# Where the expert sums, dots and weight loads stand around a phase change, in a fused attention and product-key expert kernel

## The chip, the cores and the metric

The kernel runs on one core of a Trainium2 chip. The metric is the device time of one execution in microseconds. The core has a matrix engine (PE, whose weight loads are shown as PEld), a vector engine (DVE), an activation engine (ACT), GpSimd (POOL, which issues the indirect gathers here) and SyncE (SP, which issues nearly all other transfers). Each engine takes its instructions in the order in which they were recorded, and waits on semaphores for the others.

## The reference

Two branches read the same layer-normed tokens, and their outputs are added to the input: attention with 32 query heads of width 16 on one shared key and value head, and a product-key expert layer. There are 2048 tokens of width 512.

```python
def _A_ref(x, wq, wk, wv, wo):
    q = (x @ wq).reshape(B, S, 32, 16).transpose(0, 2, 1, 3)
    k = x @ wk
    v = x @ wv
    p = softmax(einsum("bhqd,bkd->bhqk", q, k) * 16 ** -0.5)
    return einsum("bhqk,bkd->bhqd", p, v) -> (B, S, 512) @ wo

def _B_ref(x, w_q, k1, k2, u, v):
    q = einsum("nd,dhc->nhc", xf, w_q)          # 32 heads, 2 x 128 wide
    s1, s2 = q[..., :128] @ k1.T, q[..., 128:] @ k2.T   # 64 scores each
    i1, i2 = top 2 of s1, top 2 of s2           # 4 candidate pairs
    top_s, top_e = best 2 of the 4 sums         # expert i1 * 64 + i2 of 4096
    g = softmax(top_s)
    act = gelu(einsum("nd,nhkd->nhk", xf, u[top_e]))
    return einsum("nhk,nhk,nhkd->nd", g, act, v[top_e])

xn = layernorm(x)
return x + _A_ref(xn, ...) + _B_ref(xn, ...)
```

So each token meets 64 experts (32 heads, 2 each). An expert needs a row of u for a dot with the token, a gelu, and a row of v for a weighted sum.

## The kernel before

**Tokens.** The 2048 tokens stand in four groups of 512 (phases 0 to 3), each of four tiles of 128. The 32 expert heads are taken in eight chunks of four.

**Attention** is the backbone. 256 double steps, counted by `d`, each do for one unit (a block of 512 queries and four heads) two key tiles: four score tiles (`scores`, L326, and the exp on ACT, L329) and two `pv` products (L340). Into each double step the kernel puts two kinds of other work, by `att_steps(d, mid, fill)`.

**The search** is the filler on PE (`fill`). `score_thread` is a generator that walks the list `SEQ` of (phase, chunk): all chunks of phase 0, two chunks of phase 1, all of phase 2, the other six of phase 1, all of phase 3. `item` scores one token tile against one chunk: twelve matmuls into a PSUM tile `psc` (L531), then on DVE eight MAX8 (L544) and eight index finds (L546), which free that tile. `psc`, `pw`, `pwt`, `pact`, `pout`, `pwo`, `pg` and `ptd` share three PSUM buffers. Each `yield` gives a cost in planned microseconds, and `run_scores` takes steps until the plan (`aim`, growing evenly over the double steps) is met.

**Chunk weights.** In phase 0, beside the search of chunk n, `wp_make` builds the weights of chunk n + 1: per head a raw tile `wqt` is loaded by SP (`wp_load`), multiplied by the keys (`pw`, L486), copied by ACT, and transposed by PE (`pwt`, L493); ACT makes the high part (L495), DVE the low part `wk` (L496), which also frees the transpose's PSUM tile. The weights are stored to DRAM (`dw`) and read back in later phases (`wp_read`). Where the phase changes, the four tiles `xt` of transposed tokens are reloaded by SP during the last token tile of the old phase (`load_phase2_xt`).

**Slots (phases 0 and 1).** For these tokens the experts' rows are gathered: 512 slots, each a POOL gather `g` of 128 rows of u and v together (L970), a dot on DVE with the tokens (`dots`, L982) and a weighted sum on DVE into the token's accumulator `xa` (`adds`, L1017). For each four slots there is a chain of three small operations on DVE (`gq`, `gy`, `ga`; the list `CHAIN`), a tanh on ACT (`gth`, L998) and a weight on DVE (`w`, L1005). Twelve buffers hold gathers (`NGB`), two of them lent at times to the output weights (`lent`). A sum frees its gather buffer, and the next gather may start.

**Dense groups (phases 2 and 3).** For these tokens all 4096 experts are multiplied on PE, in 32 blocks (`dense`). The gates of the found experts are spread from one-hot products: `batch` makes `da` tiles of indices and gates (the gates come last, after an exp on ACT: `den`, L635, to `da`, L643, put into the list `BEHIND`), PE transposes them (`ptd`, L752), DVE makes one-hots (L777 to L780) and PE multiplies these (`pg`, L809). Then each block has `pact` (L727), an activation, and `pout` (L855). `dense_on` tells the stage: 4 at the last token tiles of the search ahead of a dense group, 2 for the one-hots, 3 and 1 for the blocks.

**The order by hand.** The loop over d sets how many dots are recorded in this double step: `pos` grows by a rate that depends on the stage, and `todo` is what is due, as far as gathers were issued. `mid`, recorded between the attention products of the double step, has in this order: the tanhs that are ready, the ACT lists, the dots (with one weight ahead of the last dot), and then `go`: the sums, the rest of `BEHIND` (`rest`) and `CHAIN` in turn, and up to four gathers. `fill` follows: the search's steps of that double step. While `dense_on` is 2, `go` is recorded after the filler instead (`POST_FILL`), with the chain at once. `quiet` counts double steps in which no sum is recorded; before, only the end of the one-hots set it.

Of the kernel before, what the change touches and what calls it, by code (L numbers as in the profile page):

```python
# [11 lines left out]
F32 = mybir.dt.float32  # L12
# [11 lines left out]
P = 128  # L24
# [31 lines left out]
def tile_kernel(ctx, tc, x, wq, wkv, wo, wqT, kT, uv, ub, vb, out):  # L56
# [408 lines left out]
    def wp_load(c, h):  # L465
        if late[0] is None or (c == 1 and h < 2):
            w = gtile(F32, (P, 2, D), "wqt") if c == 0 and h > 1 else big.tile([P, 2, D], F32, name="wqt", tag="wqt", bufs=2)
        else:
            w = late[0].tile([P, 2, D], F32, name="wqt", tag="gy", bufs=3)
        nc.sync.dma_start(w, wqT[4 * c + h].rearrange("(s p) d -> p s d", p=P))  # L470
        WC["raw", c, h] = w

# [3 lines left out]
    def wp_make(c):  # L476

        wt = [big.tile([P, 2, 512], F32, name="wt", tag="da", bufs=2) for _ in range(2)]
        for h in range(4):
            for n in range(4 * c + h + 1, min(4 * c + h + 3, 4 * NC) if late[0] else 4):  # L480
                if ("raw", n // 4, n % 4) not in WC:
                    wp_load(n // 4, n % 4)
            w = WC.pop(("raw", c, h))
            p = xtile("pw")
            for s in range(2):
                nc.tensor.matmul(p[s * E:(s + 1) * E, :], kTs[:, s, :], w[:, s, :], start=True, stop=True)  # L486
            nc.scalar.copy(wt[h // 2][:, h % 2, :], p)
            yield 0.9
        WC[c] = []
        for k in range(KC):  # L490
            p = xtile("pwt")
            for h in range(4):
                nc.tensor.transpose(p[:, h * P:(h + 1) * P], wt[h // 2][:, h % 2, k * P:(k + 1) * P], ident)  # L493
            wk = wk_tile()
            nc.scalar.copy(wk[:, 0, :], p)  # L495
            nc.vector.tensor_tensor(out=wk[:, 1, :], in0=p, in1=wk[:, 0, :], op=OP.subtract)  # L496
            WC[c].append(wk)
            store(lambda k=k, wk=wk: nc.sync.dma_start(d_w[c][:, k], raw(wk[:])))
            yield 0.45
# [12 lines left out]
    def item(n_, ti, make=()):  # L512
        ph, c = SEQ[n_]
        nph, nc_ = SEQ[n_ + 1] if n_ + 1 < len(SEQ) else (None, None)
        t = TPH * ph + ti
        g, j = divmod(t, GT)
        b, jb = divmod(ti, BT)
        if jb == 0:
            m8 = small.tile([P, BT, 8, 8], F32, name="m8", bufs=1)
            i8 = small.tile([P, BT, 8, 8], U32, name="i8", bufs=1)  # L520
            M8[ph, c, b], I8[ph, c, b] = m8, i8
        m8, i8 = M8[ph, c, b], I8[ph, c, b]
        p = xtile("psc")

        last = ti == TPH - 1
        more = nc_ is not None and not (ph >= NSP and c == NC - 1)
        read = more and n_ + 1 >= NC
        n = 0
        for k in range(KC):
            for a, bb in TERMS:  # L530
                nc.tensor.matmul(p, XT[g][k][:, a, j * P:(j + 1) * P], WC[n_][k][:, bb, :],  # L531
                                 start=n == 0, stop=n == 11)
                n += 1
            if read and ti == 0 and k < 2:
                wp_read(n_ + 1, range(2 * k, 2 * k + 2))
            if last and more and nph != ph:
                load_phase2_xt(nph, k)
            if k < KC - 1:
                yield 3 * UNIT
            if k == 1:  # L540

                yield from islice(make, 1)
        for s in range(8):
            nc.vector.max(m8[:, jb, s, :], p[:, s * E:(s + 1) * E])  # L544
        for s in range(8):
            nc.vector.max_index(i8[:, jb, s, :], m8[:, jb, s, :], p[:, s * E:(s + 1) * E])  # L546
        if jb == BT - 1:
            batch(ph, c, b)
        yield 3 * UNIT
# [100 lines left out]
    def dense(DG, after):  # L650
# [211 lines left out]
        for b in range(NB):  # L862
            wd = []
            if b > 1:
                if b not in halved:

                    yield None
                if b not in halved:
                    flush()
                p = xtile("pact")  # L870
                for k in activations(b, splits[b][0], p):
                    if k == 0:
                        store(lambda b=b: fetch_gates(b + 1))
                        if b % 2 == 0 and b > 2:
                            later_split(b + 2)
                        if b == 2:

                            store(load_totals)
                    if k == KC - 1 and b == NB - 1 and after is not None:
                        wp_read(after, range(2))  # L880
                    if b == NB - 1 and after is not None:
                        load_phase2_xt(SEQ[after][0], k)
                    if k < KC - 1:
                        yield 3 * UNIT

                if b not in fetched:
                    if b > 3 and formed[0] < b - 2:
                        flush()
                    run(STORES)
                    assert b in fetched  # L890
            vs = splits.pop(b)[1]
            gy = gates[b]
            if b > 2:
                gates.pop(b - 1)
            g, y = (gy[:, 0, :], gy[:, 1, :]) if b > 1 else (gy[:, b, :], hh[:, b, :])

            def gated(g=g, p=None):
                stt(g, g, 1.0 / GS, p, op0=OP.mult, op1=OP.mult)

            def whole(y=y, g=g):  # L900
                stt(y, y, 1.0, g, op0=OP.add, op1=OP.mult)

            def scaled(y=y, g=g):
                multiplied[0] += 1
                stt(g, g, 1.0 / GS, y, op0=OP.mult, op1=OP.mult)

            def high(y=y if b > 1 else g, wd=wd):
                wd.append(late[0].tile([P, 2, 512], F32R, name="wd", tag="wd", bufs=4))
                nc.scalar.copy(wd[0][:, 0, :], y)
                behind(lambda: low(y, wd[0]))  # L910

            def low(y, wd):
                nc.vector.tensor_tensor(out=wd[:, 1, :], in0=y, in1=wd[:, 0, :], op=OP.subtract)  # L913
                formed[0] += 1

            if b > 1:
                nc.scalar.activation(y, p, AF.Square, scale=C_CUB ** 0.5)
                stt(y, y, C_IN, p, op0=OP.add, op1=OP.mult)
                LAST.append(lambda y=y: nc.scalar.activation(y, y, AF.Tanh))
                if b == 3:  # L920

                    behind(lambda gated=gated, g=g, p=p: gated(g, p))
                else:
                    gated(g, p)
                behind(whole)
                LATER_ACT.append(high)
            else:
                LATER.append(lambda scaled=scaled, high=high: (behind(scaled), on_act(high)))
            held.append((wd, vs))
            if b > 1:  # L930
                yield 3 * UNIT
            if b == 3:
                later_split(4)
            if b == 4:
                dense_on[0] = 1
            for _ in range(b - 1 if b in (2, 3) else 0):
                if out_ready():
                    block_out()
                    yield 3.6
            if b % 2:  # L940
                if b > 1:
                    later_split(b + 2)
                if ready:
                    for _ in range(2):
                        if formed[0] < used[0] + 2:
                            yield None
                    yield from sums()
                ready, held = held, []
# [140 lines left out]
    def score_thread():  # L1089
        for n, (ph, c) in enumerate(SEQ):  # L1090
# [7 lines left out]
            for ti in range(TPH):  # L1098
                if dn and ti == 1:
                    yield next(dn)  # L1100
                if dn and ti == 2:
                    dense_on[0] = 4
                yield from item(n, ti, make)
                yield from islice(make, 1)
# [31 lines left out]
    def att_steps(d, mid, fill):  # L1136
# [41 lines left out]
        if i == STEPS + 2:  # L1178
            last_out_a(3)
            last_out_b()  # L1180
        if i >= 124 and i % 128 == 124 or i == STEPS - 30:
            lent[0] = 2
        if 128 <= i < STEPS and i % 128 == (26 if i // 128 == 2 else 10) or i == STEPS - 10:
            load_wo()
# [57 lines left out]
    with tc.manual_schedule(engines={E_.PE, E_.Activation, E_.DVE, E_.Pool, E_.SP}):  # L1242
# [3 lines left out]
        for d in range(half + 24):  # L1246
# [4 lines left out]
            if dense_on[0] == 1:  # L1251
                pos += 2.6 if d < half * 3 // 4 else max(0.0, NSL - pos) / max(half - 3 - d, 1)
            else:
                pos += (2.1 if len(IDX) < NC * TPH else 2.3 if 0 <= d - since < 12 else 1.75, 0, 1.4, 1.5, 0.5)[dense_on[0]]

            todo = max(min(int(pos + 0.001), g_next[0]) - d_next[0], 0)

            def mid():
# [23 lines left out]
                if quiet[0] > 0:  # L1282
                    quiet[0] -= 1
                    sums = 0
                if dense_on[0] == 2:
                    run(CHAIN)

                def go():
# [14 lines left out]
                        if OUTS:  # L1303
                            experts_out(OUTS.pop(0))

                if dense_on[0] == 2:
                    POST_FILL.append(go)
                else:
                    go()
# [56 lines left out]
```

## Time and profile before

| | |
|---|---|
| median of 3 runs | 1934.66 us (1933.02, 1934.66, 1942.46) |
| profiled execution | 1943.82 us, span 1942.1 us |
| mean granted TensorE clock | 0.978 |
| PE busy | 1870.5 us, 96% |
| DVE busy | 1675.0 us, 86% |
| ACT busy | 1294.5 us, 67% |
| POOL busy | 562.6 us, 29% |
| transfers | 491.11 MB, mean 253 GB/s |

Times in the rows are microseconds from the start of the span. A row of a table of stretches gives for one stretch its length, the busy time of PE, PEld, DVE, ACT and POOL with the number of their instructions, the clock granted to PE (1.00 is full speed), the busy share of the transfer engines and their rate. A row of waits names who waited, for whom, the total, the number and the longest. A row of the instructions in order of time gives start, length, engine, line, operation, tiles and count, and in brackets the idle time before it and who ended it. A group's row gives busy time and mean ns, and then the idle time before.

The double steps begin at about 139 us. Chunk weights are made until about 377, the phases change near 377, 424, 1097 and 1250 us, the search of phase 2 ends and its dense group begins near 610, and the dense group of phase 3 begins near 1437.

### The profile page before, as it was taken

What the parts mean: (1) busy time and instruction counts of PE and PEld (TensorE: products, weight loads), DVE (VectorE), ACT (ScalarE), POOL (GpSimd) and SP (SyncE); (2) the same over time, 40 slices, a digit from 0 to 9 for tenths busy, and PEclk for the clock granted to TensorE, in tenths of its full rate; (3) what the DMA queues carried; (4) which work ended last, traced back from release to release, by engine and by line L of the source; (5) the groups of instructions that cost most, each with busy time, mean ns of one, the idle gap of its engine ahead of it and who ended that gap; (6) DMA issues with size and microseconds to landing.
All of it is one profiled execution on the core that took longest, in us unless ns stands there. A gap on an engine that the chain in (4) does not pass through costs nothing.

```text
span 1942.1 us, 34774 instructions
## 1 busy us (share of the span) xinstructions
PE 1870.5 (96%) x10990; PEld 994.7 (51%) x10990; DVE 1675.0 (86%) x6717; ACT 1294.5 (67%) x1803; POOL 562.6 (29%) x536
## 2 busy tenths in 40 slices
PE   6879999999999999999999999999999999999998
PEld 4634444555554544555555554555555445555553
DVE  6627788989999986899999897999999779999994
ACT  3236666655556887778778555655578877788873
POOL 1202223222221222344344423222212124344430
PEclk9979999999999889999999999999999899999999
DMA  7857879787773667798899988777746778989882
GB/s 272 316 178 257 276 269 305 278 299 239 235 254 106 197 223 244 247 287 286 276 281 299 375 284 262 256 236 260 235 126 223 240 227 279 286 265 297 279 276 84
DMA packets 234393, 491.11 MB, mean 253 GB/s; under 512 B 93396, under 2 KB 93396, under 8 KB 234204
## 3 DMA queue, kind: packets, MB, share of 16 engines
q0 software_dynamic: 73728, 268.47, 41.8%
q1 hardware_dynamic: 159240, 219.56, 34.9%
q8 instruction: 88, 1.44, 0.3%
q10 hardware_dynamic: 1236, 0.82, 0.1%
q14 instruction: 101, 0.83, 0.1%
HBM read 427.41 MB, written 56.07 MB: 249 GB/s over the span
## 4 chain that ended last, share of the span: by engine, by line
PE 70%; DVE 17%; ACT 2%; DMA 2%; issue 1%; SPq 0%; another core or an unknown queue 0%; ACTq 0%; DVEq 0%
PE pv L340 20%; PE sc L326 14%; PE psc L531 10%; PE pact L727 9%; PE pout L855 9%; DVE i L546 5%; PE pg L809 3%; DVE m L544 3%; DVE xa L1017 3%; PE pwo L433 2%; DVE g L982 2%; ACT pt L329 2%; PE pw L486 1%; DMA wqt<-in_wqT_dram 1%; DMA wk<-dw 1%
## 5 line engine op out<-in xcount | busy, mean ns | idle before, releaser
L329 ACT ACTIVATE pt<-sc 128x1024 f32<-128x1024 f32 x1024 | 993.5, 1026 | 461.2 <-PE sc L326 413.4
L970 POOL DMA_INDIRECT g<-in_uv_dram,idx x512 | 554.7, 1083 | 1325.5 <-DVE xa L1017 670.7
L340 PE MATMUL pv<-pt,vaug 128*32 128x512 f32 x4096 | 513.1, 619 | 0.0
L531 PE MATMUL psc<-wk,xt 128*128 128x512 f32 x1536 | 390.7, 402 | 9.5 <-DVE wk L496 2.9
L326 PE MATMUL sc<-qa,kaug 64*128 64x512 f32 x2048 | 386.7, 453 | 9.6 <-ACT pt L329 8.8
L1017 DVE SCALAR_TENSOR_TENSOR xa<-g,w,xa 128x512 f32<-128x512 f32 x512 | 372.5, 746 | 0.1
L982 DVE CUSTOM_DVE_ANT_0 g<-g,xa 128x512 f32<-128x512 f32 x512 | 335.5, 682 | 6.6 <-DMA g<-in_uv_dram,idx 6.6
L531 PEld LDWEIGHTS psc<-wk,xt 128*128 128x128 f32 x1536 | 278.2, 188 | 114.5 <-issue 38.0
L326 PEld LDWEIGHTS sc<-qa,kaug 64*128 64x128 f32 x2048 | 157.0, 186 | 331.5 <-ACT pt L329 205.7
L340 PEld LDWEIGHTS pv<-pt,vaug 128*32 128x32 f32 x4096 | 109.3, 111 | 256.4 <-issue 254.8
L546 DVE FIND_INDEX8 i<-m,psc 128x8 uint32<-128x64 f32 x1024 | 206.6, 222 | 0.0
L727 PE MATMUL pact<-xt,wk 128*128 128x512 f32 x768 | 197.6, 402 | 1.5 <-DVE i L546 1.1
L855 PE MATMUL pout<-wk,wd 128*128 128x512 f32 x768 | 194.9, 402 | 0.2 <-DVE wd L913 0.2
L544 DVE MAX8 m<-psc 128x8 f32<-128x64 f32 x1024 | 146.3, 215 | 27.6 <-PE psc L531 26.1
L727 PEld LDWEIGHTS pact<-xt,wk 128*128 128x128 f32 x768 | 140.0, 189 | 51.1 <-issue 17.9
L855 PEld LDWEIGHTS pout<-wk,wd 128*128 128x128 f32 x768 | 140.8, 188 | 47.4 <-DVE act L982 4.7
L692 DVE TENSOR_TENSOR wk<-rw,wk 128x512 fp32r<-128x512 f32 x128 | 85.0, 684 | 8.0 <-ACT wk L691 8.0
L858 DVE TENSOR_TENSOR da<-da,pout 128x512 f32<-128x512 f32 x128 | 82.9, 681 | 10.1 <-PE pout L855 9.4
L777 DVE TENSOR_TENSOR oh<-oh 128x2048 f16<-128x2048 f16 x64 | 78.0, 1219 | 2.2 <-PE pg L809 2.2
L809 PEld LDWEIGHTS <-oh 128*128 128x128 f16 x1024 | 68.4, 163 | 13.1 <-issue 4.6
L809 PE MATMUL pg<-oh 128*128 128x32 f16 x1024 | 73.6, 247 | 0.4 <-DVE oh L780 0.4
L691 ACT CAST wk<-rw 128x512 fp32r<-128x512 f32 x128 | 74.0, 631 | 0.0
(156 smaller groups left out, 1286.6 us busy)
## 6 DMA issues: line engine op xcount, KB each, us to landing
wk<-dw SPq DMA_DIRECT2D x96, 512.0 KB
wqt<-in_wqT_dram SPq DMA_DIRECT2D x32, 512.0 KB
dw<-wk SPq DMA_DIRECT2D x32, 512.0 KB
rw<-in_ub_dram SPq DMA_DIRECT2D x64, 256.0 KB
rw<-in_vb_dram SPq DMA_DIRECT2D x64, 256.0 KB
gy<-dg SPq DMA_DIRECT2D x64, 256.0 KB
qa<-dqh SPq DMA_DIRECT2D x128, 64.0 KB
g<-in_uv_dram,idx POOLq DMA_INDIRECT x512
```

Source lines behind the costliest of these rows:

```text
L326: nc.tensor.matmul(p[:, b, :], kaug[o:o + 64, kc * P:(kc + 1) * P], QA[u][o:o + 64, i, :], start=True, stop=True)
L329: nc.scalar.activation(pt, p, AF.Exp, scale=SCALE)
L340: nc.tensor.matmul(PV[u][32 * j:32 * j + 32, :], vaug[:, kc, :], pt[:, b, :], start=kc == 0, stop=kc == 15)
L531: nc.tensor.matmul(p, XT[g][k][:, a, j * P:(j + 1) * P], WC[n_][k][:, bb, :], start=n == 0, stop=n == 11)
L544: nc.vector.max(m8[:, jb, s, :], p[:, s * E:(s + 1) * E])
L546: nc.vector.max_index(i8[:, jb, s, :], m8[:, jb, s, :], p[:, s * E:(s + 1) * E])
L727: nc.tensor.matmul(p, us[:, a, k * P:(k + 1) * P], XT[DG][k][:, c, :], start=n == 0, stop=n == 11)
L809: nc.tensor.matmul(p[:, i * NB:(i + 1) * NB], oa[:, :, i], ob[:, :, i], start=True, stop=True)
L855: nc.tensor.matmul(p, wd[0][:, a, j * P:(j + 1) * P], vs[:, c, :], start=n == 0, stop=n == 5)
L970: nc.gpsimd.indirect_dma_start(out=gt, out_offset=None, in_=uv, in_offset=bass.IndirectOffsetOnAxis(ap=IDX[ph, c, ti][:, s:s + 1], axis=0))
L982: nc.vector.tensor_tensor_reduce(u, u, XN[TPH * ph + ti], scale=1.0, scalar=0.0, op0=OP.mult, op1=OP.add, accum_out=a[:, i:i + 1])
L1017: nc.vector.scalar_tensor_tensor(acc, v, w[:, i:i + 1], acc, op0=OP.mult, op1=OP.add)
```

## The change

- `wp_load`: the later raw weight tiles use the four buffers of the tag `wd` in place of three of `gy`, and `wp_make` asks for them up to three heads ahead, not two.
- `item`: at the last but one token tile before the phase changes (other than to a dense group's blocks), `quiet` is set to 3: no sums for three double steps. `dense` does the same at the first step of its last block, if a phase follows.
- `score_thread`: stage 4 starts one token tile earlier, and its rate of slots is 0, not 0.5. In `mid`, stage 4 records the rest of `BEHIND` (the gates) ahead of the sums, and at most one sum.
- While the search is in phase 0 (fewer than 32 entries in `IDX`), the chain is recorded right behind the dots and `go` (sums, gates, gathers) after the filler, as in stage 2. The rate of slots there is 2.3, not 2.1.
- `pos` may not run more than one slot ahead of the gathers. The lending of two gather buffers ahead of the second load of `wo` moves from step 252 to 272 (double step 126 to 136).

```diff
@@ wp_load, wp_make
-            w = late[0].tile([P, 2, D], F32, name="wqt", tag="gy", bufs=3)
+            w = late[0].tile([P, 2, D], F32, name="wqt", tag="wd", bufs=4)
...
-            for n in range(4 * c + h + 1, min(4 * c + h + 3, 4 * NC) if late[0] else 4):
+            for n in range(4 * c + h + 1, min(4 * c + h + 4, 4 * NC) if late[0] else 4):
@@ item
+        if ti == TPH - 2 and more and nph != ph:
+            quiet[0] = 3
@@ dense, a block's activations
+                    if k == 0 and b == NB - 1 and after is not None:
+                        quiet[0] = 3
@@ score_thread
-                if dn and ti == 2:
+                if dn and ti == 1:
                     dense_on[0] = 4
@@ att_steps
-        if i >= 124 and i % 128 == 124 or i == STEPS - 30:
+        if i >= 124 and i % 128 == 124 and i // 128 != 1 or i == 272 or i == STEPS - 30:
             lent[0] = 2
@@ the loop over d
-                pos += (2.1 if len(IDX) < NC * TPH else 2.3 if 0 <= d - since < 12 else 1.75, 0, 1.4, 1.5, 0.5)[dense_on[0]]
+                pos += (2.3 if len(IDX) < NC * TPH else 2.3 if 0 <= d - since < 12 else 1.75, 0, 1.4, 1.5, 0)[dense_on[0]]
+            pos = min(pos, g_next[0] + 1.0)
@@ mid
-                if dense_on[0] == 2:
+                if dense_on[0] == 4:
+                    run(rest)
+                    sums = min(sums, 1)
+                if dense_on[0] == 2 or len(IDX) < NC * TPH:
                     run(CHAIN)
...
-                if dense_on[0] == 2:
+                if dense_on[0] == 2 or len(IDX) < NC * TPH:
                     POST_FILL.append(go)
                 else:
                     go()
```

## The prediction

> **What bounds the kernel.** I read the page's busy shares first, then a table of the stretches between the places where the matrix engine pauses, then the waits of PE inside those stretches.
>
> ```profile
> PE   1870.5 (96%) x10990; PEld 994.7 (51%) x10990; DVE 1675.0 (86%) x6717; ACT 1294.5 (67%) x1803; POOL 562.6 (29%) x536
> ```
> ```profile
> core 0: us, PE busy (x) PEld busy (x) DVE busy (x) ACT busy (x) POOL busy (x), PEclk, DMA share, GB/s
> 146.00:377.00 231.00, 222.29 (x1287) 106.85 (x1279) 190.74 (x1022) 150.25 (x201) 63.09 (x63) 1.00 0.80 272
> 418.00:436.00 18.00, 15.67 (x84) 7.96 (x86) 15.52 (x99) 8.09 (x10) 4.03 (x4) 0.91 0.87 316
> 436.00:582.00 146.00, 145.54 (x828) 80.90 (x821) 140.48 (x926) 84.37 (x104) 36.40 (x36) 1.00 0.75 244
> 606.00:620.00 14.00, 10.08 (x53) 5.28 (x49) 11.20 (x44) 7.76 (x13) 4.76 (x4) 0.76 0.56 146
> 620.00:713.00 93.00, 92.42 (x812) 47.15 (x808) 84.12 (x171) 74.36 (x124) 16.98 (x14) 0.85 0.56 186
> 1083.00:1103.00 20.00, 18.19 (x101) 10.15 (x103) 14.95 (x59) 8.83 (x12) 8.22 (x8) 1.00 1.04 367
> 1103.00:1152.00 49.00, 49.00 (x286) 27.05 (x288) 47.68 (x287) 28.91 (x36) 13.83 (x14) 1.00 0.89 316
> 1398.00:1442.00 44.00, 39.60 (x235) 22.45 (x234) 42.10 (x261) 25.91 (x36) 10.07 (x10) 1.00 0.43 135
> 1442.00:1542.00 100.00, 97.15 (x910) 51.76 (x912) 95.18 (x195) 87.25 (x144) 24.57 (x20) 0.93 0.67 218
> 1542.00:1899.00 357.00, 356.27 (x1986) 190.66 (x1979) 321.42 (x750) 278.39 (x395) 136.47 (x122) 1.00 0.86 270
> ```
>
> PE is the bound: it is busy 96% of the span, and the instruction lists of the two programs have the same 3305 rows on PE in the same order, and the same on POOL. So the change can only move when PE waits. The table says where that is: 8.7 us idle (231 less 222.3) while chunk weights are made, 2.3 at the second token change, 3.9 where the first dense group begins, 1.8 where it ends, 4.4 where the second begins. Together 21 us, plus the halved clock (0.91 and 0.76). In long stretches between, PE has no idle time, but DVE runs at 96% (140.5 of 146) and 97% (47.7 of 49): there is no room there for DVE work pushed in from elsewhere.
>
> **Part 1, chunk weights (146 to 377).** PE's waits in that stretch, then DVE ahead of the longest:
>
> ```profile
> PE psc L531 <- DVE wk L496: 2.9, 3, 1.6
> PE pwt L493 <- DVE i L546: 2.3, 1, 2.3
> PE pw L486 <- DMA wqt<-in_wqT_dram: 1.9, 1, 1.9
> PE pw L486 <- issue: 1.1, 1, 1.1
> PE psc L531 <- issue: 0.6, 1, 0.6
> ```
> ```profile
> 312.26 2.07 DVE L1017 SCALAR_TENSOR_TENSOR xa<-g,w,xa 128x512 f32<-128x512 f32 x3
> 314.25 1.14 DVE L544 MAX8 m<-psc 128x8 f32<-128x64 f32 x8
> 317.13 0.63 PE L493 MATMUL pwt<-ident,wt 128*128 128x128 f32 x4 [2.27 <-DVE i L546]
> ```
>
> DVE takes its list in order. Three sums (L1017, 2.07 us) stood ahead of the search (MAX8, then the index finds) whose end frees the PSUM tile that PE's transpose needs. In the new order the sums are recorded after the filler, behind the search and L496, so the search can begin 2.07 earlier and the 2.3 falls to 0.2. The other waits here on DVE's search and weight split (the 1.1 put down to issue begins while DVE is still in that chunk's index finds) are shorter than those 2.07, except one of 1.6 in which L496 itself waited for ACT; that one stays. 2.9 + 2.3 + 1.1 + 0.6 - 1.6 = 5.3 can go; sums are not ahead of every search (some double steps have one), so I take 4.0, with 0 and 5.3 as ends. The 1.9 on wqt: the raw weights are now asked for three heads ahead, in four buffers, so each load stands one head earlier on SP; a pw pair and its filler last longer than 1.9, and I take all of it (ends 0 and 1.9). On SP the runs of these loads stay in place, the first one load longer and the last one shorter; so the load at each run's border passes a chunk's stores and a set of q loads, which start one 0.5 MB load later; no wait of PE above is on them, so zero. The few other moves on SP (rw, gy, rsb and an out store, by a place or two) I also take as zero: no row here shows a wait on them.
>
> The pace goes from 2.1 to 2.3 slots per double step. Stepping the code's counters through (they hold no time), 71 dots are out at double step 31 against 65, and the lead is 7 by step 34. A slot costs DVE a dot, a sum and a quarter of the factor chain and the weight:
>
> ```profile
> L1017 DVE SCALAR_TENSOR_TENSOR xa<-g,w,xa 128x512 f32<-128x512 f32 x512 | 372.5, 746 | 0.1
> L982 DVE CUSTOM_DVE_ANT_0 g<-g,xa 128x512 f32<-128x512 f32 x512 | 335.5, 682 | 6.6 <-DMA g<-in_uv_dram,idx 6.6
> ```
>
> 0.75 + 0.68 + about 0.15 = 1.6 us, times 7 = 11 us. DVE goes from 190.7 to 202 of 231, 87%: hidden, since DVE at 96% in the next stretch leaves PE without waits. The factor chain at once (three short operations) moves 0.5 us ahead of the search and feeds the tanh earlier; zero. What is late next there is ACT: the exps and the weight casts, which the change does not move.
>
> **Part 2, token changes.** Transfers at the second one (422 to 427), PE's waits on them there and at the dense group's end, the size of gathers, and slices of 3.4 us:
>
> ```profile
> 422.81 1.02 SPq L1086 DMA_DIRECT2D xt<-dxt  x2
> 423.02 1.20 POOL L970 DMA_INDIRECT g<-in_uv_dram,idx  x1 [13.24 <-DVE xa L1017]
> 425.78 0.94 POOL L970 DMA_INDIRECT g<-in_uv_dram,idx  x1 [0.30 <-DVE i L546]
> ```
> ```profile
> PE psc L531 <- DMA xt<-dxt: 2.3, 1, 2.3
> PE psc L531 <- DMA wk<-dw: 1.8, 2, 1.3
> ```
> ```profile
> q0 software_dynamic: 73728, 268.47, 41.8%
> ```
> ```profile
> 428.40:431.80 3.40, 1.07 (x5) 0.56 (x4) 3.13 (x11) 0.96 (x2) 0.15 (x1) 1.00 1.00 335
> 431.80:435.20 3.40, 3.40 (x11) 2.28 (x11) 2.74 (x24) 0.00 (x0) 0.79 (x1) 0.56 1.01 406
> ```
>
> Three sums free three gather buffers, and three gathers (268.47 MB by 512 = 0.52 MB each) start beside the last two token tiles. With sums held for three double steps, these 1.57 MB come later: at 335 GB/s that is 4.7 us of the transfers' time, more than the 2.3 of wait on xt. I take 1.8 (ends 0 and 2.3). The halved clock after it cost (1 - 0.56) x 3.4 = 1.5 us; I take 1.2. At the dense group's end the wait is on wk (1.8, transfers at share 1.04); there the counters withhold 8 sums, so 8 gathers, 4.2 MB or over 10 us of transfers: I take 1.3 (0 to 1.8). (Of the two rows on PE's waits the first is of 418 to 436, the second of 1083 to 1103.) At the first and the fourth token change no wait of PE on a transfer stands among those above: zero.
>
> **Part 3, a dense group's beginning.** PE and DVE at the first, its slices (and one at the second), and a wait of PE at the second:
>
> ```profile
> 614.26 1.11 PE L752 MATMUL ptd<-ident,da 128*128 128x128 f32 x4 [2.73 <-DVE da L643]
> 609.70 1.41 DVE L1017 SCALAR_TENSOR_TENSOR xa<-g,w,xa 128x512 f32<-128x512 f32 x2
> 611.62 0.68 DVE L982 CUSTOM_DVE_ANT_0 g<-g,xa 128x512 f32<-128x512 f32 x1
> 612.24 0.75 DVE L1017 SCALAR_TENSOR_TENSOR xa<-g,w,xa 128x512 f32<-128x512 f32 x1
> 612.90 0.26 DVE L635 TENSOR_SCALAR den<-ex 128x16 f32<-128x16 f32 x1
> ```
> ```profile
> 610.20:613.60 3.40, 0.66 (x4) 0.42 (x4) 3.33 (x9) 1.17 (x2) 2.27 (x3) 0.93 0.38 73
> 613.60:617.00 3.40, 2.74 (x9) 2.36 (x10) 3.10 (x8) 0.59 (x1) 2.49 (x2) 0.50 0.91 278
> 617.00:620.40 3.40, 3.40 (x19) 1.13 (x21) 1.32 (x4) 2.43 (x4) 0.00 (x0) 0.57 1.05 268
> 1398.40:1401.80 3.40, 2.10 (x10) 1.38 (x8) 3.40 (x25) 0.96 (x2) 2.15 (x2) 1.00 0.74 195
> ```
> ```profile
> PE psc L531 <- DVE i L546: 1.6, 1, 1.6
> ```
>
> PE waits for the last gates (den to da). The dot at 611.62 is gone (no slots), the sum at 612.24 falls behind the gates, and one of the two at 609.70 is cut: 1.28 + 0.67 = 1.95 of the 2.73, and the dot cut at two steps before takes the short wait ahead (0.5): 2.4 of 3.9 (ends 0 and 3.9). The clock at half then cost (0.50 + 0.43) x 3.4 = 3.2 us. A stretch of 3.4 us with 2.10 us of PE work kept its clock, those with 0.66 and 1.07 lost it; with 1.95 less waiting the stretch has about 2.6: I take 2.5 (0 to 3.2). At the second beginning PE idles 4.4; the 1.6 of the last row, on a search at 1400, comes before the edit acts and stays. Of the other 2.8 (gates, a search, a one-hot) I take 2.0 for two dots and two sums less (0 to 2.8).
>
> The Trainium skill, "TensorE: Matmul & The Clock Gate", section "What's actually happening", has the clock fall only after an idle window of about 3.4 us. This trace does not agree as far as it shows: no single wait here reaches 3.4, and the clock fell after 2.33 and after 2.73. Read strictly, the falls would have another cause, the 1.2 and 2.5 would not come, and the sum would be 11.4.
>
> **What comes back.** Withheld work returns where DVE is full. In 436 to 582 the counters give 5 sums more, 3.7 us, into 5.5 of slack; in 1103 to 1152, 4 more, 3.0 us, into 1.3. I charge 2.0 in all; ends 0 and 8.5 (both wholly, plus 1.8 for a tile's sum recorded late). The second dense group starts 3 slots behind: 4.8 us into the 35.6 of slack in 1542 to 1899, zero. The lending of two gather buffers moves from double step 126 to 136, which leaves the gathers their full depth around the dense group's end: zero. The new cap on the pace only keeps it from running ahead of the gathers: zero.
>
> **Sum.** 4.0 + 1.9 + 1.8 + 1.2 + 1.3 + 2.4 + 2.5 + 2.0 - 2.0 = 15.1 us. The profiled execution took 1943.82 us (span 1942.10), 9.2 above the median of 1934.66; what an execution adds to the median may be just these halved clocks, so of the 3.7 of clock I count half against the median: 13.3, or 1921 us. All upper ends together are 22.7 us (1912); none with the full return is 1943.
>
> **Rivals.** (a) DVE's backlog decides, and it is slower: the sums withheld at the token changes return in the stretches at 96 and 97%, PE waits for searches there, and the earlier waits shrink little. It decides once more DVE work than their slack of 5.5 and 1.3 (6.8 us) is pushed into them and the gains fall under that; for it speaks how small the slack is, against it that 7 slots are done earlier. The full return of 8.5, 3.7 more from its searches and 2 of gain: 10 us over, 1945. Chance 0.17. (b) Waits change their owner: behind DVE stands ACT (65% busy in the first stage, in order too), the transfers are late anyway (share 0.87 and 1.04), and a third to half of the sum is left: 1928 to 1931, within 0.5%. Chance 0.23. (c) All ends, and the halved clocks of the one-hot stages shrink as well (0.15 of 93 us and 0.07 of 100, 21 us that the program does not touch but whose phase shifts): a third of that on top of most ends, 1909. Chance 0.12. (d) The clock falls stay though the gaps shrink, because at these places PE has too little work in a window anyway: without the 3.7 the sum is 11.4, 1923. Chance 0.08. That is what the Trainium skill's rule (same page and section) comes to. The forecast itself has 0.40, its own range 1914 to 1927.
>
> **Chances.** 0.5% (9.7 us) is about what a measurement of this kernel can tell from no change. Faster by more (below 1925): most of the forecast (0.33), (c), three quarters of (d) and a little of (b) (0.02): 0.53. Within: 0.31. Slower by more (above 1944.3): most of (a), 0.16. The range 1907 to 1943 leaves out the far end of (a) and of (c).
>
> **What would show it.** Right: in the stretch of chunk weights no wait of PE on DVE over 1 us and none on wqt, and the step to the second token change comes some 6 us earlier; gathers begin after the xt tiles have landed; the wait on da (L643 before) under 1 us and PEclk 1.00 in the stretch after it. Wrong: PE waits on searches in the two full stretches, DVE waiting for psc in every double step of the first stage with sums behind it, dots waiting for gathered rows, or the same falls of the clock without gaps.

## The result and the profile after

The changed kernel takes 1951.9 us (median of 7 runs, 1947.76 to 1956.67), the kernel before 1936.62 us (7 runs, 1927.82 to 1943.45). The ratio is 1.0079 with an interval of 1.0054 to 1.0104: slower by 0.8%, where 1921 us and a gain were forecast.

The page of the changed kernel, busy shares, and a table of its stretches (columns as in the table of before):

```profile
PE 1869.4 (96%) x10990; PEld 995.1 (51%) x10990; DVE 1675.5 (86%) x6717; ACT 1293.5 (66%) x1803; POOL 560.3 (29%) x536
```
```profile
146.00:375.00 229.00, 222.73 (x1290) 107.25 (x1292) 198.11 (x1037) 151.16 (x202) 71.37 (x67) 1.00 0.82 282
417.00:434.00 17.00, 13.89 (x70) 7.24 (x69) 12.09 (x84) 7.85 (x9) 2.27 (x3) 0.85 0.98 351
434.00:583.00 149.00, 143.58 (x809) 79.23 (x811) 140.05 (x917) 80.80 (x100) 37.98 (x37) 0.99 0.71 237
596.00:606.00 10.00, 8.19 (x38) 3.57 (x37) 9.86 (x70) 6.63 (x9) 2.04 (x3) 0.83 0.35 105
606.00:626.00 20.00, 19.24 (x128) 10.25 (x127) 14.91 (x76) 15.23 (x22) 2.27 (x3) 1.00 0.38 108
626.00:707.00 81.00, 80.00 (x782) 44.44 (x784) 78.08 (x161) 72.09 (x121) 16.82 (x14) 0.95 0.57 191
1080.00:1097.00 17.00, 17.00 (x100) 9.53 (x102) 7.13 (x16) 8.39 (x10) 3.08 (x3) 1.00 0.90 346
1097.00:1160.00 63.00, 56.20 (x308) 29.89 (x300) 57.82 (x345) 31.46 (x39) 23.20 (x22) 0.97 0.78 274
1400.00:1446.00 46.00, 43.32 (x268) 23.84 (x264) 41.07 (x256) 28.80 (x38) 8.19 (x8) 1.00 0.41 136
1446.00:1550.00 104.00, 101.72 (x908) 52.15 (x904) 94.08 (x196) 87.38 (x146) 20.14 (x18) 0.88 0.60 198
```

The work is the same, and the places where PE pauses have changed. Some old pauses are gone: at the dense group's end (1080 to 1097) PE now has no idle time, and behind the first dense beginning (606 to 626) the clock is full. In their place PE idles 5.4 us in the stretch from 434 to 583 (0.5 before, 436 to 582) and 6.8 us in 1097 to 1160 (none before, 1103 to 1152). These two stretches were the ones in which DVE was full.

Who waits there: first the waits of PE and then of DVE in 434 to 583.

```profile
PE psc L533 <- DVE i L548: 5.3, 3, 3.2
DVE g L986 <- DMA g<-in_uv_dram,idx: 3.2, 1, 3.2
DVE den L608 <- ACT ex L585: 2.1, 1, 2.1
DVE m L546 <- PE psc L533: 0.7, 1, 0.7
```

And in 1097 to 1160:

```profile
PE sc L326 <- ACT pt L329: 4.2, 3, 3.5
PE psc L533 <- DVE i L548: 1.1, 2, 0.7
DVE g L986 <- DMA g<-in_uv_dram,idx: 4.6, 2, 4.1
```

DVE waits for gathered rows, which it did not do in either stretch before. In 434 to 583 it waits 3.2 us for one, and PE waits as long for a search 27 us later:

```profile
457.95 0.69 DVE L986 CUSTOM_DVE_ANT_0 g<-g,xa 128x512 f32<-128x512 f32 x1 [3.17 <-DMA g<-in_uv_dram,idx]
488.35 0.98 PE L533 MATMUL psc<-wk,xt 128*128 128x512 f32 x3 [3.18 <-DVE i L548]
```

Behind the first of these rows DVE has no wait left in the stretch, so what it is late at 458 stays in its list until PE needs a search. PE's other two waits there (1.5 and 0.7, at 539 and 561) come from the same full list later on. The 2.1 on an exp (`den`, at 439) does not explain them by itself: the last version below waits 2.3 us for the same exp, and PE has no idle time behind it. In the second stretch the chain can be followed in the order of time, DVE, ACT and PE, with the transfer that began it (from the chain of work that ends there):

```profile
1106.99 8.68 DMA g<-in_uv_dram,idx
```
```profile
1115.69 0.69 DVE L986 CUSTOM_DVE_ANT_0 g<-g,xa 128x512 f32<-128x512 f32 x1 [4.10 <-DMA g<-in_uv_dram,idx]
1126.19 0.15 DVE L996 SCALAR_TENSOR_TENSOR gy<-gq,act 128x4 f32<-128x4 f32 x1
1126.37 0.21 ACT L1002 ACTIVATE gth<-gy 128x4 f32<-128x4 f32 x1 [7.55 <-DVE gy L996]
1127.65 0.50 PE L326 MATMUL sc<-qa,kaug 64*128 64x512 f32 x2 [3.48 <-ACT pt L329]
```

A gather lands 8.68 us after its start, longer than a double step. The dot waits 4.1 us for it, the factor chain behind the dots ends late, the tanh of these factors stands in ACT's list ahead of the exps and makes ACT wait 7.55 us, and PE waits 3.5 us for an exp to free its score tile.

One remark on the two profiled executions. They differ by 7.4 us (1951.25 and 1943.82), the medians by 15.3, mostly because the profile of before lies 7.2 above its own median. Half clock where the one-hots are multiplied explains less than 5 of these: at the first dense group 0.85 of full speed over 93 us before against 0.95 over 81 us here (14 and 4 us lost), but at the second 0.93 over 100 us before against 0.88 over 104 us here (7 and 12). What else made that execution slow is not known. The idle times of PE compared above do not rest on it.

### The profile page after: what moved, and what is told of

Read it like the earlier page. It is cut to its first block, busy times and chain, and to the rows that moved or that the text cites. A ratio compares the mean times of both kernels' runs of the same rounds, so it can differ in the third digit from the quotient of the medians.

```text
span 1949.5 us, 34780 instructions
## 1 busy us (share of the span) xinstructions
PE 1869.4 (96%) x10990; PEld 995.1 (51%) x10990; DVE 1675.5 (86%) x6717; ACT 1293.5 (66%) x1803; POOL 560.3 (29%) x536
## 4 chain that ended last, share of the span: by engine, by line
PE 62%; DVE 24%; DMA 3%; issue 3%; ACT 2%; SPq 0%; POOL 0%; ACTq 0%; DVEq 0%; POOLq 0%
PE pv L340 18%; PE sc L326 12%; PE pact L729 9%; PE pout L857 9%; PE psc L533 7%; DVE i L548 6%; DVE xa L1021 5%; DVE m L546 4%; DVE g L986 3%; PE pg L811 2%; PE pwo L433 2%; DMA g<-in_uv_dram,idx 2%; ACT pt L329 2%; PE pw L486 1%; DVE oh L779 1%
## 5 line engine op out<-in xcount | busy, mean ns | idle before, releaser
L974 POOL DMA_INDIRECT g<-in_uv_dram,idx x512 | 552.4, 1079 | 1335.5 <-DVE xa L1021 693.8
L533 PE MATMUL psc<-wk,xt 128*128 128x512 f32 x1536 | 393.5, 403 | 17.6 <-DVE i L548 10.7
L860 DVE TENSOR_TENSOR da<-da,pout 128x512 f32<-128x512 f32 x128 | 83.0, 680 | 10.9 <-PE pout L857 10.7
```

The source lines that it names most:

```text
L974: nc.gpsimd.indirect_dma_start(out=gt, out_offset=None, in_=uv, in_offset=bass.IndirectOffsetOnAxis(ap=IDX[ph, c, ti][:, s:s + 1], axis=0))
```

## The experiments

The first question was which edit costs the time. Theory R: the withheld sums and their late gathers. Theory P: the first stage's order and pace, which put sums into another step of the search.

**Without the quiet edits.**

```diff
 # the changed kernel
-        if ti == TPH - 2 and more and nph != ph:
-            quiet[0] = 3
...
-                    if k == 0 and b == NB - 1 and after is not None:
-                        quiet[0] = 3
```

> The changed kernel without its two quiet edits (sums are never withheld at a token change or at a dense group's last block). Theory R (return): the loss comes from the sums that quiet withholds, which return three to a double step, and from the gathers that start late for it. Then the waits of PE on DVE's searches of 3.2 us near 485 and on ACT of 3.5 us near 1124 are gone, and the ratio to the kernel before is 0.993 to 1.000. Theory P (phase): the loss comes from the first stage's new order and faster pace, which leave the sums in another step of the search than before; then the waits near 485, 537 and 560 stay and the ratio is 1.004 to 1.008.

Measured: 1933.91 us against 1938.55, ratio 0.9968 (0.9944 to 0.9992). The same two stretches:

```profile
433.00:573.00 140.00, 140.00 (x796) 78.30 (x798) 135.62 (x905) 80.47 (x99) 32.30 (x32) 1.00 0.74 246
1094.00:1157.00 63.00, 63.00 (x359) 33.31 (x359) 61.43 (x388) 37.32 (x46) 16.81 (x16) 1.00 0.87 303
```

PE has no idle time in either. Theory R as it forecast: the quiet edits turn a gain of 0.3% into a loss of 0.8%. This run keeps every other edit, the cap on `pos` and the later lending too, so none of these makes the loss without the quiet edits.

**The quiet edits alone.** The four lines above, added to the kernel before.

> The kernel before with the two quiet edits alone. Theory R: PE waits on searches after the second token change and after the dense group's end, each 3 us or more in all; ratio 1.003 to 1.008. Theory P: the order is otherwise that of before, nothing new is late, and the shorter waits on transfers show: ratio 0.996 to 1.000.

Measured: 1969.31 us, ratio 1.0139 (1.0103 to 1.0175), worse than forecast, and worse than the whole change. In its two stretches:

```profile
442.00:592.00 150.00, 143.22 (x802) 78.29 (x800) 138.82 (x901) 80.62 (x100) 39.48 (x39) 0.99 0.70 235
1109.00:1173.00 64.00, 56.93 (x319) 30.96 (x317) 59.28 (x355) 32.30 (x41) 19.96 (x19) 0.96 0.88 310
```

PE idles 6.8 and 7.1 us. Why it is worse than the whole change was not tested. The gains of the other edits are missing here, and at 1195 us PE waits 5.5 us for DVE ahead of an output product (`PE pwo L433 <- DVE xa L437`), which the changed kernel does not.

**The first stage's order alone.**

```diff
 # the kernel before
-                if dense_on[0] == 2:
+                if dense_on[0] == 2 or len(IDX) < NC * TPH:
                     run(CHAIN)
...
-                if dense_on[0] == 2:
+                if dense_on[0] == 2 or len(IDX) < NC * TPH:
                     POST_FILL.append(go)
```

> The kernel before with the first stage's order alone (chain at once, sums and gates behind the filler while phase 0 is searched; pace 2.1 and the load of raw weights as before). Theory R: 0 to 3 us gained between 146 and 377, the waits on DVE's searches there of 2.3 and 1.1 shorter by up to 2; ratio 0.997 to 1.000. Theory P: as much, but PE waits on DVE after 377 that were not there; ratio 1.001 to 1.005.

Measured: 1936.73 us, ratio 0.9983 (0.996 to 1.0006). This can't be told from no change, and theory P's loss of 0.1 to 0.5% (1.001 to 1.005) lies outside the interval.

**The edits at a dense group's beginning alone.** `ti == 1` for `ti == 2`, the rate 0 for 0.5, and in stage 4 `run(rest)` ahead of at most one sum.

> The kernel before with the edits at a dense group's beginning alone (stage 4 one token tile earlier, no slots in it, gates ahead of at most one sum). Both theories: the wait of PE for the last gates falls from 2.7 to under 1 us at the first beginning and from 1.5 to under 1 at the second; ratio 0.996 to 1.000. Theory P adds that the 3 to 4 slots lost are a new phase for all that follows, so new waits of PE on DVE of 1 to 3 us may stand behind it.

Measured: 1948.01 us, ratio 1.0044 (1.0022 to 1.0066): slower, which neither theory had. At both beginnings the wait on the gates is gone as forecast, but at the dense group's end, far behind the edit, PE waits longer than before (1.8 there):

```profile
PE psc L531 <- DMA wk<-dw: 4.2, 1, 4.2
```

A guess is that the slots dropped at the beginning are missing there. It is tested further down, by giving them back through the pace.

**Late gathers or bunched sums?** Withholding sums does two things: it brings sums back three to a double step, and it takes away the gathers' lead over the dots, because a gather needs the buffer that a sum frees. Counted in the traces, as the gathers that POOL has started less the dots that DVE has started, the lead around the second token change is 6 to 8 before and falls to 0 in the changed kernel; at the dense group's end it is 4 to 7 before and 0 to 4 after. In the changed kernel POOL starts no gather for 29 us:

```profile
419.02 0.94 POOL L974 DMA_INDIRECT g<-in_uv_dram,idx  x1 [0.30 <-DVE m L546]
448.33 1.39 POOL L974 DMA_INDIRECT g<-in_uv_dram,idx  x1 [28.37 <-DVE xa L1021]
```

Theory B lays the loss to the bunching, theory D to the lost lead.

Gathers are recorded later, sums are not withheld:

```diff
 # the kernel before, hold[0] = 3 set where quiet was set
+                held = hold[0] > 0
+                hold[0] -= held
...
-                    gathers(4)
+                    if not held:
+                        gathers(4)
```

> The kernel before, with gathers (not sums) withheld for three double steps at the places where the change withholds sums. Up to the first dense group the sums and dots stand as before; only the gathers' lead over the dots falls from 8 to 2. Theory B (bunching: three sums in a row of double steps make DVE late): no wait of PE on searches between the second token change and the first dense group, ratio 0.998 to 1.003. Theory D (depth: the gathers start late, DVE waits for rows, and what is behind the dot in its list is late): DVE waits for gathers by 4 us or more there, PE waits on searches by 3 or more, ratio 1.005 to 1.012.

Measured: 1948.17 us against 1943.53, ratio 1.0017 (1.0002 to 1.0033), which is in theory B's range. At the second token change, behind it, and behind the dense group:

```profile
404.00:432.00 28.00, 28.00 (x161) 15.37 (x160) 25.40 (x168) 15.72 (x18) 5.04 (x6) 1.00 0.75 270
432.00:573.00 141.00, 140.49 (x798) 78.38 (x798) 138.04 (x916) 80.65 (x99) 36.35 (x36) 1.00 0.77 255
1097.00:1162.00 65.00, 58.12 (x319) 30.95 (x317) 59.80 (x348) 32.19 (x41) 21.86 (x21) 0.97 0.79 272
```

Theory D's figures for the first stretch did not come, but the edit did not do there what it was meant to do. The first gather behind the loads of xt:

```profile
423.39 1.21 POOL L974 DMA_INDIRECT g<-in_uv_dram,idx  x1 [13.24 <-DVE xa L1021]
```

It starts as soon as a sum has freed its buffer, as in the kernel before (423.02), and so do the next two (424.90 and 426.16, before 424.53 and 425.78). Recorded later, they start no later, and the lead stays 6 to 8. So the first stretch tests neither theory, and the wait at the change itself (2.3 before), which is gone here, did not go because gathers were held. Behind the dense group the edit does act, in another way: the program records no dot ahead of its gather, so DVE starts no dot from 1071 to 1090 and no sum from 1079 to 1102. Then dots and sums come four at a time, the lead falls to 2 three times, DVE waits 4.3 us for gathered rows, and PE idles 6.9 us. Sums are late and bunched there as well, so this does not part the theories either.

The quiet edits with the sums returned slowly:

```diff
 # the kernel before, with the quiet edits
                 if quiet[0] > 0:
                     quiet[0] -= 1
                     sums = 0
+                    paced[0] = 16
+                elif paced[0] > 0:
+                    paced[0] -= 1
+                    sums = min(sums, 2)
```

> The kernel before with the two quiet edits, and after each the sums return at no more than two to a double step. Theory B: the waits of PE on searches after the token changes go (under 2 us in all between the second and the first dense group); ratio under 1.006. Theory D: the gathers' lead stays at 2 for longer, so the waits of DVE on gathers grow; ratio 1.014 or more.

Measured: 2084.05 us, ratio 1.0728 (1.0695 to 1.0761). In its stretch behind the second token change the waits of PE and DVE are

```profile
PE psc L533 <- DVE i L548: 16.6, 4, 6.0
PE sc L326 <- ACT pt L329: 6.7, 3, 3.3
DVE g L986 <- DMA g<-in_uv_dram,idx: 31.2, 17, 5.0
```

No sums three to a double step, a lead of 0 to 3 that stays (so counted in the trace from 386 to 617 us), and the loss is five times that of the plain edits. Bunching as the only cause is contradicted; theory D fits. The 7% is of the whole kernel, whose other stretches are slower too.

Sums bunched, nothing withheld:

```diff
 # the kernel before
+                if 40 <= d < 60:
+                    sums = min(a_ready[0] - a_next[0], 4) if d % 2 == 0 else 0
```

> The kernel before, with the sums between double steps 40 and 60 bunched: up to four in one double step, none in the next. No transfer is withheld, and the gathers' lead over the dots stays between 5 and 11. Theory B (bunched sums make DVE late for PE): PE waits on searches by 3 us or more between the second token change and the first dense group. Theory D (the gathers' lead decides): under 1 us of such waits, no wait of DVE on gathers, ratio 0.998 to 1.003.

Measured: 1940.09 us, ratio 0.9995 (0.9975 to 1.0015), and

```profile
439.00:580.00 141.00, 140.47 (x800) 78.20 (x798) 137.97 (x908) 80.60 (x99) 37.70 (x36) 1.00 0.75 254
```

0.5 us idle on PE, as without the edit. Four sums in one double step, with none in the next, are harmless while the lead is 6 to 9. (What five double steps of three sums each add to a DVE that is already late was not isolated.)

**One double step of quiet** in place of three, in the changed kernel (`quiet[0] = 1` at both places).

> The changed kernel with one double step without sums in place of three. The gathers' lead over the dots then stays at 6 or more at the token changes and 4 or more behind the dense group. Theory D: DVE waits for gathers under 1 us in both stretches, the loss is gone: ratio 0.995 to 1.001. If any withholding costs in proportion: a third of the 1.1% between the changed kernel and the one without quiet, ratio 1.000 to 1.003.

Measured: 1932.94 us, ratio 0.9969 (0.9949 to 0.999). PE's stretches are full again, 141 of 141 and 63 of 63:

```profile
430.00:571.00 141.00, 141.00 (x806) 78.54 (x806) 138.03 (x922) 80.90 (x100) 35.03 (x35) 1.00 0.74 249
1086.00:1149.00 63.00, 63.00 (x363) 33.26 (x355) 62.21 (x390) 37.74 (x47) 19.31 (x19) 1.00 0.82 295
```

The loss is not in proportion to the withheld sums: it is gone, as theory D has it. The lead counted in the traces, around the second token change and around the dense group's end, stands beside PE's idle time in the full stretch behind each:

| run | lead | PE idle, us | lead | PE idle, us |
|---|---|---|---|---|
| kernel before | 6 to 8 | 0.5 | 4 to 7 | 0 |
| changed kernel | 0 to 5 | 5.4 | 0 to 4 | 6.8 |
| without quiet | 5 to 9 | 0 | 4 to 8 | 0 |
| quiet alone | 0 to 4 | 6.8 | 2 to 4 | 7.1 |
| quiet, slow return | 0 to 2 | 23.4 | 2 to 3 | 10.7 |
| bunched sums | 6 to 9 | 0.5 | 4 to 7 | 0 |
| quiet of one | 5 to 8 | 0 | 2 to 7 | 0 |

(Counted at each dot from 10 us ahead to 40 us behind the start of the first stretch, and from 25 us ahead to 30 us behind that of the second.) The stretches of the slow return are longer, 178 and 125 us. Where PE idles 5 us or more, the lead is nowhere over 5 and falls to 2 or less; a lead of 2 to 4 for some 20 us ahead of the second stretch, in the last row, leaves that stretch full, although DVE waits 4.6 us for rows ahead of it (1060 to 1086).

**Stage 4 with the pace.** The stage 4 edits, and the rate 2.3 for 2.1.

> The kernel before with the stage 4 edits and the first stage's pace of 2.3. If the stage 4 edits alone were slower because the three or four slots that they drop make the tokens' last sums late at the first dense group's end, the lead of the pace pays for these: the wait of 4.2 us on the token tiles near 1090 goes and the ratio is 0.995 to 1.000. If they were slower for their order (gates ahead, one sum), it stays at 1.003 to 1.006.

Measured: 1934.48 us against 1943.53, ratio 0.996 (0.9939 to 0.9982). At the dense group's end PE is busy again:

```profile
1075.00:1097.00 22.00, 21.36 (x125) 11.43 (x127) 18.82 (x93) 12.52 (x16) 7.93 (x8) 1.00 1.03 375
```

With the pace the wait on wk is 0.3 us: the stage 4 edits are 0.4% slower without it and 0.4% faster with it. How the slots act on the load of wk was not followed, and the pace alone was not run, so its own share is not known. (The expectation speaks of a wait on token tiles; the row of the run before names wk.)

**Versions put together.** The order, the raw weights and the gates ahead, without the pace:

> The kernel before with the first stage's order, the earlier raw weights, and in stage 4 the gates ahead of at most one sum, without the pace, the dropped slots and the quiet. Sum of what the single runs showed: 2 to 4 us from the order, 1.9 from the raw weights, 1 to 2 from the gates: ratio 0.994 to 0.998, and no wait of PE on the load of raw weights. If the places are not independent (transfers at the first dense group's end shift again), 0.998 to 1.002.

Measured: 1942.79 us, ratio 0.9996 (0.9975 to 1.0017): no gain that can be told, where 0.2 to 0.6% was expected; what came is the alternative named there. The gains read off single rows did not add up. And two with pace and stage 4, the earlier raw weights, and gathers held at token changes, without and with the first stage's order:

> A version put together: the kernel before with the stage 4 edits, the pace of 2.3, the earlier raw weights, and gathers (not sums) withheld for three double steps at the token changes alone. The wait on the token tiles at the second change, 1.5 us without it, goes, and so does the half clock behind it; ratio 0.992 to 0.997.

> The same with the first stage's order as well (chain at once, sums behind the filler). With the order 1 to 2 us less than without it, as it was worth alone: ratio 0.991 to 0.997; if order and pace stand in each other's way, 0.996 to 1.000.

Measured: 1933.28 us, ratio 0.9974 (0.9952 to 0.9995), and 1933.56 us, ratio 0.9971 (0.9947 to 0.9994). Neither is told apart from the version without quiet (0.9968) or from stage 4 with the pace alone (0.996). Both miss what was hoped for at the second token change: the wait on the token tiles that holding was to remove stayed, 1.6 us of 18 in the first and 3.2 in the second. It had to, since holding the records does not hold the gathers (as shown above). The row of the first:

```profile
415.00:433.00 18.00, 16.38 (x92) 8.70 (x94) 17.17 (x106) 8.51 (x11) 4.96 (x5) 1.00 0.88 300
```

So five of the versions beat the kernel before by 0.3 to 0.4%. All five hold the stage 4 edits and the pace of 2.3, and at both places their lead keeps to 4 or more, but for the spell of 2 to 4 in the version with one double step of quiet. The kernel before keeps its lead too, so the lead is not what makes them faster than it.

## Why the prediction was wrong

**The step that failed** is "What comes back". It treated a withheld sum as 0.75 us of DVE work that returns into an average slack, charged 2.0 us with 8.5 as the end, and gave the later gathers, in part 2, as a gain only ("these 1.57 MB come later"). A sum also frees the buffer of a gather that a later dot waits for, and for that there was no term, although "dots waiting for gathered rows" stands among the signs of being wrong. What the runs showed in its place: POOL starts no gather for 29 us, the lead falls to 0, DVE waits for rows in both full stretches (3.2 and 4.6 us), and PE idles 11.7 us more in them (5.4 and 6.8 against 0.5 and 0). Without the quiet edits the change is faster by 0.3%, with them slower by 0.8%.

Rival (a) named the right stretches and the right sign, 1945 us. Its mechanism (returning sums crowd DVE) is at most a part. In the first stretch the returned sums do take DVE's slack: it has 140.05 us of work there, against 135.62 in the run without quiet. But with quiet alone DVE has no more work than before (138.82 against 140.48), and PE idles 6.8 us; bunched sums cost nothing, and slower return cost 7%. How much of the 5.4 us in the first stretch the returned sums would cost without the late rows was not isolated; in the second the chain of rows above leads to the late gather.

**Part 1, chunk weights.** Forecast 4.0 for the order and 1.9 for the raw weights. Waits of PE in 146 to 375 after the change:

```profile
PE psc L533 <- DVE wk L496: 3.7, 4, 1.6
PE pwt L493 <- DVE i L548: 1.5, 1, 1.5
PE pw L486 <- issue: 1.1, 1, 1.1
```

The wait on wqt (1.9) is gone, but not by the edit alone: it is gone as well in the runs with the order alone and with stage 4 and the pace, where the raw weights are loaded as before. The waits on DVE went from 6.9 to 6.3 only: the 2.3 became 1.5 in place of 0.2. The reason stands in PE's rows, of before and then, with DVE's, of after:

```profile
312.08 0.96 PE L531 MATMUL psc<-wk,xt 128*128 128x512 f32 x3
```
```profile
310.66 0.96 PE L533 MATMUL psc<-wk,xt 128*128 128x512 f32 x3
312.11 1.14 DVE L546 MAX8 m<-psc 128x8 f32<-128x64 f32 x8
314.98 0.63 PE L493 MATMUL pwt<-ident,wt 128*128 128x128 f32 x4 [1.54 <-DVE i L548]
```

Before, the search's own tile was finished at 313.04, 1.2 us ahead of its MAX8 at 314.25; so without the sums the search could begin at most 1.2 us earlier, not 2.07. It now begins 0.5 us behind the tile, the last of three dots standing ahead of it, and 0.7 us are gained. The waits on L496 did not shrink (2.9 and 0.6 put down to issue before, 3.7 now): at 275.86 L496 no longer stands behind three sums, but waits 2.1 us for ACT's cast. ACT was named there as the next to be late; it was late already, and the term was mis-sized: 0.6 for 4.0. The second token change came 1.9 us earlier (first loads of xt at 416.16, before 418.07), where some 6 were expected. The faster pace was hidden, as forecast (DVE 198 of 229).

**Part 2, token changes.** Forecast 1.8 and 1.2 at the second, 1.3 at the dense group's end. At the dense group's end the wait of 1.8 is gone (17.00 of 17.00), but it is gone as well without the quiet edits (PE has no wait from 1080 to 1094 there), so the withheld gathers were not needed for it. At the second change the wait on xt grew from 2.3 to 3.1 us and the clock fell as before (0.85 in 417 to 434). In the changed kernel three gathers start at 416 to 420, ahead of the last xt loads, where before they started at 423 to 427, and the transfers' share is 0.98; the gap in the gathers comes only behind them. That the earlier gathers made the wait longer is likely and not shown: the wait is not steady, since it is absent in the run with later records, whose loads and gathers start as in the kernel before.

**Part 3, dense beginnings.** At the first the wait on da is gone, only 0.7 on ACT is left in 606 to 626, and the clock behind it is full. But 1.4 and 0.4 us of wait on an exp stand new in 596 to 606, with the clock at 0.83. So of 3.9 us idle 2.6 are left (1.8 and 0.8), a gain of 1.3 for a forecast 2.4; and 1.7 us of clock are lost (0.17 of 10) where 3.4 were (0.24 of 14), again 1.7 for 2.5. At the second 2.7 us idle are left of 4.4: 1.7 for a forecast 2.0. That these edits lose at the dense group's end without the pace was not foreseen: three missing slots were costed at zero.

**The clock.** The Trainium skill, "TensorE: Matmul & The Clock Gate", section "What's actually happening", gives an idle window of about 3.4 us as the cause of a fall. In the changed kernel it also fell in the stretch 596 to 606, in which PE idles 1.8 us in all (8.19 busy of 10.00); its slices of 3.4 us:

```profile
596.30:599.70 3.40, 1.59 (x10) 0.53 (x12) 3.40 (x24) 3.40 (x7) 0.28 (x1) 0.97 0.50 154
599.70:603.10 3.40, 3.40 (x18) 0.74 (x12) 3.26 (x23) 0.98 (x2) 0.93 (x1) 0.52 0.00 0
```

The trace does not agree with the rule as read there. The same two waits on an exp stand in six traces, with 8.15 to 8.20 us of work in 10: the clock is 0.83 in three of them (the changed kernel, the one without quiet, and the last version) and 1.00 in the other three (stage 4 with the pace, quiet of one, and the first of the last two versions). What decides between them is open. Rival (d) did not come: where the gap ahead of the gates went, the clock rose (0.76 in 606 to 620 before, 1.00 in 606 to 626 now).

## What to carry to other kernels

Before you withhold an operation, follow what it frees: here a sum releases a buffer, a gather fills it, and a dot waits for that, 8.7 us later in the row above. Count the lead of the prefetch and not only the amount of work: here a lead that fell to 0 for several double steps cost more than the waits it was meant to remove. Before you price a wait, look when its input was ready (a search can't begin ahead of its tile), and whether the wait stands in a second run as well. Several edits to a full schedule need not add up: test a change by taking out one edit at a time, since one can turn the gain of the others. And look in the trace whether an edit moved what it was meant to move.

## What the runs showed that was not expected

- A gather whose record was moved up to three double steps later started when it did before, as soon as a sum had freed its buffer (423.39 against 423.02 us).
- A lead of 0 to 3 that lasts goes with 31 us of DVE's waits for rows behind one token change, in a kernel slower by 7% (1.0728); with quiet of one DVE also waited 4.6 us for rows, at the dense group's end, and PE had no idle time behind it.
- The tanh of the slots, four numbers per partition and 0.21 us long, waited 7.55 us on ACT for its input and held the exps that stand behind it in order; so a late gather reached PE by ACT and not only by DVE.
- The same waits of PE (1.4 and 0.4 us in a stretch of 10) left the clock full in three traces and not in three others.
- Executions of one program differ by the clock granted: in 35 of the kernel before it was 0.973 to 0.984, the slowest (1951.59 us) having the lowest and the fastest (1927.14 us) the highest.
